# A two-stage convolution with a joint on one Trainium2 core: first samples loaded by phase, warming products split, 414 direct outputs instead of 438, smaller last pieces

## The chip, the cores and the metric

The kernel runs on one core of a Trainium2 chip. The time is the device time of one launch in microseconds (us), the median of three runs. The core's engines are named as in the profile: PE (TensorE; PEld is its weight load), DVE (VectorE), ACT (ScalarE), POOL (GpSimd) and SP (SyncE, which here only issues DMAs). Engines run on their own and wait for each other by semaphores.

## The reference

Two batches of 4000 samples with 512 channels go through two convolutions of 5 taps, each with a GELU and then every second output kept. A joint follows: a product with `w_f`, a sum with a term of `g` for each of 8 labels, tanh, and a product with `w_o`.

```python
B, T, D, K = 2, 4000, 512, 5
U = 8
...
xp = jnp.pad(x, ((0,0),(pad,pad),(0,0)))
for i in range(K):
    h = h + jnp.einsum("btc,cd->btd", xp[:, i:i+T, :], w1[i])
h = _gelu(h)[:, ::2, :]
...
for i in range(K):
    f = f + jnp.einsum("btc,cd->btd", hp[:, i:i+T1, :], w2[i])
f = _gelu(f)[:, ::2, :]
fe = jnp.einsum("btd,de->bte", f, w_f)
ge = jnp.einsum("bud,de->bue", g, w_g)
j = jnp.tanh(fe[:, :, None, :] + ge[:, None, :, :])
return jnp.einsum("btud,dv->btuv", j, w_o)
```

All inputs and the output are bf16. The output has 2 x 1000 x 8 rows of 512.

## The kernel before

**How it is written.** Every operation is recorded in a plan (`Plan`, L69) with what it reads and writes. `edges` finds who must wait for whom. `schedule` (L160) then lays the operations out on the engines by estimated costs, tries up to 300 variations, and `emit` writes each engine's instructions in that order. Operations that carry a "pin" keep their order; for the others PE takes the one recorded first among those that the estimate has ready, and ACT and DVE the one that is due first. All DMAs but two at the end are issued by SP, in the order in which they are recorded. A DMA with an entry in `after` waits until an earlier one has landed, and everything behind it in SP's queue waits with it. An edit of an estimate or of an amount of work thus can move the order of the whole plan.

**First convolution, batch 0.** Its outputs are made in two ways. The first ND = 438 outputs are computed directly: `direct` (L778) multiplies each of the 5 taps, in the order `TAPS` = 0, 4, 2, 1, 3, and accumulates in PSUM banks 0, 2, 4 and 6, one bank for each block of 128 output channels. One call makes 4 x 4 products (4 blocks, 4 parts of the 512 input channels) over `hi - lo` columns. The even taps read the even samples, the odd taps the odd ones. Their input is `eo` (even and odd samples, channels on partitions). It comes from `xr`: two tiles of raw samples, in which each partition holds 4 consecutive samples of 512 channels. `load_xr` (L529) loads tile 0 (128 partitions, 512 KB) and tile 1 (`NR[1]` = 96 partitions, 384 KB). `turn(rt, pp)` (L600) transposes the samples of phase pp (0 even, 1 odd) of tile rt on PE, eight transposes in two groups, and DVE or ACT copies each group from PSUM into `eo`. The first NH = 254 columns need tile 0 alone, so the even taps are split: columns 0 to NH, and NH to ND.

The next outputs of batch 0, and all of batch 1, are made by `Triple` (L661): three outputs together by 9 products instead of 15, from sums and differences of samples and of weights. These sums are made by ACT and DVE (`step` for samples, `w1part` for weights). `Unit` (L711) runs the products of one block of 128 channels of one triple. The first triple covers NF = 186 groups of three outputs, the second NL = 336; ND / 3 + NF + NL is 668 in all. The triples' samples are loaded with a transpose in the DMA, one for each of 6 phases: `xa` for the first (`load_a`, L556, 192 rows in each), `xp` for the others.

**Order of the start.** SP issues `xr` tile 0, `w1` tap 0, `w1` tap 4, then (when tile 0 has landed) `xr` tile 1, then (when tap 0 has landed) `w1` tap 2, `xa` phases 4 and 0, (when tap 4 has landed) `w1` tap 1, `xa` phase 2, (when tile 1 has landed) `w1` tap 3, the other `xa` phases, and then 18 `xp` loads. PE runs NWARM = 7 products over a tile of zeros (`warm_mm`, L591), whose result nobody reads, while the first samples are on their way. Then come the transposes, the direct products, and the units of the triples. `w1part` of DVE begins when taps 0 and 4 are there.

**The end.** The joint's last product is made in blocks of 128 rows. Most blocks go in groups of four by a scheme of seven products (`Seven`, L1086); single blocks left over go by `Plain` (L1063), which multiplies, copies from PSUM (`evict`) and stores. The last lines (L1284 to L1290) run one plain block, the first half (256 columns) of another, the last product `p4` of the last `Seven`, a plain block, and the second half of the other, whose store ACT issues. The program ends when all stores have landed.

Of the kernel before, what the change touches and what calls it, by code (L numbers as in the profile page):

```python
# [12 lines left out]
P = 128  # L13
# [355 lines left out]
def bass_standalone__seq2seq_rnn_t_joint__speech_kernel(  # L369
# [22 lines left out]
    NK = D // P  # L392
    assert (B, T, D, K, U) == (2, 4000, 512, 5, 8)
    T1, T2 = T // 2, T // 4
    NT3 = (T2 + 2) // 3
    ND, NF = 438, 186
    NL = 2 * NT3 - ND // 3 - NF
    assert ND % 6 == 0 and NF % 2 == 0 and NL % 2 == 0
    EW = 16 + 4 * P
# [3 lines left out]
    RING, WIDE, XB = 16, 10, 32  # L403
    BU = B * U
    NT = 512
    NWARM = 7
    TAPS = (0, 4, 2, 1, 3)
    NX = 2

    with ExitStack() as es:  # L410
        cur = [16512]

        def at(name, shape, dtype, offset=None):
            o = cur[0] if offset is None else offset
            b = Buf(nc, name, shape, dtype, o)
            if offset is None:
                cur[0] = (b.end + 31) // 32 * 32
            return b
# [10 lines left out]
        wo_sb = at("wo_sb", [NK, D], BF16)  # L429
        h_off = cur[0]  # L430
        hT = [at(f"hT{b}", [6, NK, HWID], BF16) for b in range(B)]
        xr = [Buf(nc, f"xr{i}", [4, NK, P], BF16, h_off + 16384 + i * 4096) for i in range(NX)]
# [10 lines left out]
        ident = at("ident", [P], BF16)  # L443
# [23 lines left out]
        ost = [at(f"ost{i}", [NT], BF16, h_off + 12288 + i * 1024) for i in range(3)]  # L467
# [13 lines left out]
        ps = Psum(es.enter_context(nc.psum_tensor("acc", [P, 8 * NT], FP32)))  # L481
        block = es.enter_context(nc.Block(no_gpsimd_drain=True))
        pl = Plan(nc)
        sub, add = ALU.subtract, ALU.add

        def vec_cost(o, ins, fast=True):
            bf = fast and all(not v.psum and v.ap.dtype in (BF16, FP16) for v in (o,) + tuple(ins))
            return o.ap.free_size() * (0.52e-3 if bf else 1.04e-3) + 0.065
# [8 lines left out]
        def act(o, i, func, scale=1.0, bias=None):  # L497
            rd = (i,) if bias is None else (i, bias)
            pl.op("act", lambda e: e.activation(o.ap, i.ap, func, scale=scale,  # L499
                                                bias=0.0 if bias is None else bias.ap), rd, (o,),  # L500
                  o.ap.free_size() * 0.833e-3 + (0.05 if i.psum else 0.105 if bias is None else 0.186))

        def mm(o, pairs, start, stop, check=True):

            def fn(e):
                for n, (l, r) in enumerate(pairs):
                    ins = e.matmul(o.ap, lhsT=l.ap, rhs=r.ap, start=start and n == 0,  # L507
                                   stop=stop and n == len(pairs) - 1, skip_group_check=not check)
                return ins
            pl.op("pe", fn, [v for pr in pairs for v in pr], (o,), len(pairs) * max(o.ap.free_size() / 2400 + 0.0028, 0.056))  # L510
# [13 lines left out]
        def load_w(eng, dst, src, slack=0.0):  # L524
            return pl.dma(eng, lambda e: e.dma_start(dst.ap, src), (), (dst,), slack=slack)  # L525

        NR = (P, 16 * -(-(2 * ND + 2 - 4 * P) // 64))

        def load_xr(rt, after=None):  # L529
            n = NR[rt]  # L530
            dst = xr[rt].rows(0, n).map(lambda a: a.rearrange("p r k c -> p (r k c)"))
            src = x[0, 4 * P * rt:4 * (P * rt + n), :].rearrange("(p r) c -> p (r c)", r=4)
            o = pl.dma("sp", lambda e: e.dma_start(dst.ap, src), (), (dst,), nbytes=n * 4096, rate=370e3)  # L533
            if after is not None:
                o.after.append(after.idx)
            return o
# [5 lines left out]
            src = x.rearrange("b t d -> (b t) d")[r0:r0 + 6 * (n - 1) + 1:6, :]  # L542
            return pl.dma("sp", lambda e: e.dma_start_transpose(out=dst.ap, in_=src), (), (dst,), nbytes=n * 2 * D, rate=175e3, slack=slack)

        came = [load_xr(0)]
        act(warm[0:1], warm[1:2], ACT.Gelu_apprx_tanh)

        def load_w1(i, after=None):
            o = load_w("sp", w1_sb[i], w1[i].rearrange("(k c) d -> c k d", c=P))
            if after is not None:  # L550
                o.after.append(after.idx)
            return o
# [3 lines left out]
        def load_a(*phs):  # L556
            for ph in phs:
                load_x6(xa, 0, ph, JA, 0, 16 * -(-(NF + 2) // 16), 0.8)

        came.append(load_w1(TAPS[0]))  # L560
        came.append(load_w1(TAPS[1]))
        came.append(load_xr(1, came[-3]))
        came.append(load_w1(TAPS[2], came[-3]))
        load_a(4, 0)
        came.append(load_w1(TAPS[3], came[-3]))
        load_a(2)
# [24 lines left out]
        def warm_mm(n):  # L591
            z, zz = zero[0:P], zero[:]
            for i in range(n):
                mm(ps.cols(0, NT), [(z, zz)], True, True)
                pl.ops[-1].cost = 0.43

        warm_mm(NWARM)
        psb = ps.h[:, :].bitcast(BF16)

        def turn(rt, pp, cost):  # L600
            n = NR[rt]
            for h in range(2):
                bk = 4 * (rt ^ pp) + 2 * h + 1
                pv = View(psb[:, bk * 1024:bk * 1024 + 4 * n].rearrange("p (r k c) -> p r k c", r=2, k=2), np.array([bk]), True)

                def fn(e, pv=pv, h=h):
                    for k in range(2):
                        for r in range(2):
                            ins = e.transpose(pv.ap[:, r, k, :], xr[rt].h[0:n, 2 * r + pp, 2 * h + k, :], ident.h[0:n, 0:n])  # L609
                    return ins  # L610
                pl.op("pe", fn, (xr[rt][:], ident[:]), (pv,), cost)
                lo = 16 + 2 * P * rt
                o = eo[pp, 2 * h:2 * h + 2, lo:lo + 2 * n].map(lambda a: a.rearrange("p k (c r) -> p k c r", r=2))
                v = pv.map(lambda a: a.rearrange("p r k c -> p k c r"))
                if h or rt:
                    act(o, v, ACT.Copy)
                else:
                    pl.op("dve", lambda e, o=o, v=v: e.tensor_copy(out=o.ap, in_=v.ap), (v,), (o,), vec_cost(o, (v,)))
# [157 lines left out]
        NH = 2 * P - 2  # L776

        def direct(i, lo=0, hi=ND):  # L778
            for m in range(NK):
                mm(ps.cols(2 * m * NT + lo, hi - lo),  # L780
                   [(w1_sb[i, k, m * P:(m + 1) * P], eo[i % 2, k, 15 + i // 2 + lo:15 + i // 2 + hi]) for k in range(NK)],
                   i == TAPS[0] and lo == 0, i == TAPS[-1], False)

        def h_edges(b):
            memset(hT[b][4:6, :, HOFF - 1:HOFF])
            memset(hT[b][:, :, HOFF + NT3:HOFF + NT3 + 2])

        pl.pin = False
        h_edges(0)
        turn(0, 0, 0.43)  # L790
        direct(TAPS[0], 0, NH)
        turn(0, 1, 0.43)
        direct(TAPS[1], 0, NH)
        turn(1, 0, 0.17)
        turn(1, 1, 0.17)
        direct(TAPS[2], 0, NH)
        for i in TAPS[:3]:
            direct(i, NH, ND)
        for i in TAPS[3:]:
            direct(i)  # L800
        for m in range(NK):
            v = ps.cols(2 * m * NT, ND).map(lambda a: a.rearrange("p (q r) -> p r q", r=6))
# [123 lines left out]
        def slot(j):  # L926
            if j < XB:
                return jT, j % RING
            j = (j - XB) % (WIDE + RING)
            return (jX, j) if j < WIDE else (jT, j - WIDE)  # L930
# [8 lines left out]
        def jcols(k, lo, n):  # L939

            buf, j = slot(lo // JB)
            lo = j * JB + lo % JB
            return buf[k, lo:lo + n]
# [82 lines left out]
        H = NT // 2  # L1026

        def take():
            return free.pop(0)

        def evict(eng, o, v):
            if eng is None:
                n = o.ap.free_size()
                pl.flex({"act": (lambda e: e.activation(o.ap, v.ap, ACT.Copy), 0.05 + n * 0.833e-3),  # L1034
                         "dve": (lambda e: e.tensor_copy(out=o.ap, in_=v.ap), 0.065 + n * 1.04e-3)}, (v,), (o,))  # L1035
            elif eng == "act":
                act(o, v, ACT.Copy)
            else:
                pl.op("dve", lambda e: e.tensor_copy(out=o.ap, in_=v.ap), (v,), (o,), vec_cost(o, (v,)))
# [12 lines left out]
        def store(jt, src, key, eng="sp", cl=slice(0, NT)):  # L1052
            lo = c0 = jt * P
            while lo < c0 + P:
                vv = lo // T2
                n = min((vv + 1) * T2, c0 + P) - lo
                b, u, t = vv // U, vv % U, lo % T2
                s = src(lo - c0, lo - c0 + n)
                dst = out[b, t:t + n, u, cl]
                pl.dma(eng, lambda e, s=s, dst=dst: e.dma_start(dst, s.ap), (s,), (), sem_of(key), 2 * n * P * 4)  # L1060
                lo += n

        class Plain:  # L1063
# [8 lines left out]
            def go(self, eng=None):  # L1072
                self.part(slice(0, NT), eng, "sp")

            def half(self, h, eng, queue):
                self.part(slice(h * H, (h + 1) * H), eng, queue)

            def part(self, cl, eng, queue):
                bk = take()
# [170 lines left out]
        plains = [j for j in range(ntile) if not any(q <= j < q + 4 for q in jts)]  # L1250
# [5 lines left out]
        for i, q in enumerate(seven):  # L1256
            p = seven[i - 1] if i else None
            base = min([(p or q).jt] + plains[:1]) * P
            last = i + 1 == len(seven)
            r = []  # L1260
# [23 lines left out]
        assert not conv and not pend and len(plains) == 3, (len(conv), len(pend), plains)  # L1284
        Plain(plains[0]).go()
        end = Plain(plains[2])
        end.half(0, "dve", "sp")
        seven[-1].p4(True)
        Plain(plains[1]).go()
        end.half(1, "act", "act")  # L1290

        pl.emit(block, [(s[0], s[1]) for s in sems.values()])

# [27 lines left out]
```

## Time and profile before

| | us |
|---|---|
| median of 3 runs | 252.72 (252.49 to 252.78) |
| the profiled execution | 252.61 |
| its span, first to last instruction | 250.8 |
| PE busy | 246.1 (98%) |
| ACT busy, DVE busy | 211.1, 209.4 |
| first warming product / first transpose / first direct product | 1.19 / 4.21 / 5.93 |
| first product of the first triple | 22.38 |
| last copy from PSUM starts | 247.61 |
| HBM read and written | 7.73 MB, 16.38 MB |

The span begins with the first instruction and ends with the last; the profiled time holds it and what lies around it. "Busy" of PE says that a product was in the array, not that the array was at its peak: PE's products are pipelined and their ends modelled. What an engine waits for is given by the releaser behind an arrow. A chain of waits, followed back from the last instruction, shows which work ended last at each point; work off that chain costs nothing as long as it stays off it. The weight loads (PEld) have starts that show how fast the products follow each other.

### The profile page before, as it was taken

How to read it: one execution, taken by the hardware profiler on the slowest of the kernel's cores; microseconds unless marked ns; L12 is line 12 of the kernel's file. 1: busy time of each engine (PE TensorE's matmuls, PEld its weight loads, DVE VectorE, ACT ScalarE, POOL GpSimd, SP SyncE). 2: the span in 40 equal slices, each digit the busy share in tenths (PEclk: the TensorE clock that was granted, in tenths of full speed). 3: DMA queues.
4: the chain of work that ended last, by engine and by line, in shares of the span. 5: the costliest groups of instructions: out<-in, count | busy, mean ns of one | idle time of the engine just before them, and what ended most of it. 6: DMA issues, size and time to landing. Idle time of an engine off the chain costs nothing.

```text
span 250.8 us, 5265 instructions
## 1 busy us (share of the span) xinstructions
PE 246.1 (98%) x1947; PEld 183.4 (73%) x1947; DVE 209.4 (84%) x354; ACT 211.1 (84%) x351; POOL 98.8 (39%) x106
## 2 busy tenths in 40 slices
PE   8999999999999999999999999999999999999994
PEld 4887887666666666667556878777788878787882
DVE  2699998966999999398966888777999999987783
ACT  3399998859868867884599999999999999998772
POOL 1000000000000000000006978979799899888840
PEclk9999999999999999999999999999999999999999
DMA  7999999989000043000001043423354554555456
GB/s 241 276 242 195 158 197 179 187 208 293 2 3 0 0 146 109 0 4 0 0 3 42 0 137 111 132 86 104 94 184 142 187 188 158 167 173 185 151 189 210
DMA packets 54455, 31.86 MB, mean 127 GB/s; under 512 B 31390, under 2 KB 54206, under 8 KB 54430
## 3 DMA queue, kind: packets, MB, share of 16 engines
q1 hardware_dynamic: 54142, 31.34, 47.2%
q8 instruction: 15, 0.25, 0.4%
q10 hardware_dynamic: 288, 0.20, 0.3%
q14 instruction: 10, 0.08, 0.1%
HBM read 7.73 MB, written 16.38 MB: 96 GB/s over the span
## 4 chain that ended last, share of the span: by engine, by line
PE 93%; DMA 3%; ACT 2%; DVE 1%; issue 1%; SPq 0%; DVEq 0%
PE acc L507 92%; DMA w_sb<-in_w_dram 3%; ACT row L499 1%; DVE row L494 0%; PE acc L609 0%; DVE acc L621 0%; DVE w_t L494 0%; ACT w_x L499 0%; ACT sd L499 0%; SPq L525 0%; SPq L533 0%; ACT ost L499 0%; DVE sd L494 0%; DVEq L330 0%
## 5 line engine op out<-in xcount | busy, mean ns | idle before, releaser
L494 DVE TENSOR_TENSOR og<-acc,sn 128x512 bf16<-128x512 f32 x84 | 54.9, 682 | 7.9 <-PE acc L507 7.5
L499 ACT ACTIVATE jT<-feT,geT 128x1000 bf16<-128x1000 f32 (+5 forms) x60 | 57.4, 1016 | 0.3 <-DVE feT L494 0.3
L1108 POOL TENSOR_TENSOR ss<-jT 128x512 f16<-128x512 bf16 x33 | 38.4, 1170 | 41.3 <-DVE ss L1108 41.0
L507 PE MATMUL acc<-tw,ss 128*128 128x256 f16 x336 | 46.2, 273 | 0.0
L507 PE MATMUL acc<-row,w_sb 128*128 128x334 bf16 (+2 forms) x224 | 38.9, 296 | 0.2 <-DVE acc L621 0.2
L507 PEld LDWEIGHTS acc<-tw,ss 128*128 128x128 f16 x336 | 32.3, 98 | 7.6 <-ACT sn L1034 0.6
L507 PE MATMUL acc<-wo_sb,jT 128*128 128x256 bf16 (+1 forms) x208 | 33.2, 285 | 0.0
L1034 ACT ACTIVATE sn<-acc 128x512 f32<-128x512 f32 x48 | 29.7, 628 | 3.1 <-PE acc L507 2.3
L1035 DVE COPY sn<-acc 128x512 f32<-128x512 f32 x36 | 24.6, 685 | 7.0 <-PE acc L507 6.6
L507 PEld LDWEIGHTS acc<-row,w_sb 128*128 128x128 bf16 x224 | 21.1, 97 | 9.9 <-DVE acc L621 1.4
L491 POOL MEMSET hT<- 128x8 bf16 (+2 forms) x6 | 0.8, 148 | 63.2 <-ACT hT L499 46.3
L507 PEld LDWEIGHTS acc<-wo_sb,jT 128*128 128x128 bf16 x208 | 20.3, 98 | 5.0
L499 ACT ACTIVATE sd<-acc 128x334 f32<-128x334 f32 (+2 forms) x48 | 20.5, 432 | 2.9 <-PE acc L507 1.7
L499 ACT ACTIVATE hT<-acc 128x334 bf16<-128x334 f32 (+3 forms) x36 | 15.4, 438 | 8.7 <-PE acc L507 8.4
L1108 POOL TENSOR_TENSOR ss<-ss,jT 128x512 f16<-128x512 f16 x19 | 21.9, 1156 | 0.8 <-DVE ss L1108 0.8
L621 DVE SCALAR_TENSOR_TENSOR acc<-acc,sd 128x334 f32<-128x334 f32 (+2 forms) x24 | 11.5, 479 | 9.6 <-PE acc L507 9.5
L494 DVE TENSOR_TENSOR row<-row 128x1336 bf16<-128x1336 bf16 (+2 forms) x24 | 18.8, 792 | 0.0
L499 ACT ACTIVATE jX<-feT,geT 128x1000 bf16<-128x1000 f32 (+3 forms) x20 | 18.4, 968 | 0.0
L507 PE MATMUL acc<-xp,w_t 128*128 128x334 bf16 (+1 forms) x96 | 17.6, 305 | 0.0
L507 PE MATMUL acc<-hT,w_t 128*128 128x334 bf16 x96 | 17.6, 304 | 0.0
L507 PE MATMUL acc<-wo_sb,ss 128*128 128x256 bf16 x112 | 17.3, 273 | 0.0
L507 PE MATMUL acc<-xp,w_x 128*128 128x334 bf16 (+1 forms) x96 | 16.9, 305 | 0.0
(124 smaller groups left out, 494.6 us busy)
## 6 DMA issues: line engine op xcount, KB each, us to landing
out_dram<-og SPq DMA_DIRECT2D x42, 256.0 KB, 2.5
w_sb<-in_w_dram SPq DMA_DIRECT2D x10, 512.0 KB, 5.4
out_dram<-og SPq DMA_DIRECT2D x14, 128.0 KB, 2.1
out_dram<-ost SPq DMA_DIRECT2D x10, 128.0 KB, 1.9
xr<-in_x_dram SPq DMA_DIRECT2D x1, 512.0 KB, 3.4
wf_sb<-in_w_f_dram SPq DMA_DIRECT2D x1, 512.0 KB, 3.8
wg_sb<-in_w_g_dram SPq DMA_DIRECT2D x1, 512.0 KB, 4.8
wo_sb<-in_w_o_dram SPq DMA_DIRECT2D x1, 512.0 KB, 7.2
```

What stands on the lines that cost most here:

```text
L491: pl.op("pool", lambda e: e.memset(v.ap, 0.0), (), (v,))
L494: pl.op(eng, lambda e: e.tensor_tensor(out=o.ap, in0=a.ap, in1=b.ap, op=op), (a, b), (o,), 0.02 + 2.14e-3 * o.ap.free_size() if eng == "po ...
L499: pl.op("act", lambda e: e.activation(o.ap, i.ap, func, scale=scale, bias=0.0 if bias is None else bias.ap), rd, (o,), o.ap.free_size() * ...
L507: ins = e.matmul(o.ap, lhsT=l.ap, rhs=r.ap, start=start and n == 0, stop=stop and n == len(pairs) - 1, skip_group_check=not check)
L621: pl.op(eng, lambda e: e.scalar_tensor_tensor(out=o.ap, in0=a.ap, scalar=f, in1=b.ap, op0=ALU.mult, op1=add), (a, b), (o,), vec_cost(o, (a ...
L1034: pl.flex({"act": (lambda e: e.activation(o.ap, v.ap, ACT.Copy), 0.05 + n * 0.833e-3), "dve": (lambda e: e.tensor_copy(out=o.ap, in_=v.ap) ...
L1035: "dve": (lambda e: e.tensor_copy(out=o.ap, in_=v.ap), 0.065 + n * 1.04e-3)}, (v,), (o,))
L1108: fn = lambda e, o=S[i], x=x, y=y, op=op: e.tensor_tensor(out=o.ap, in0=x.ap, in1=y.ap, op=op)
```

## The change

There are four edits.

- **Amounts.** ND is 414 instead of 438 and NF 194 instead of 186; NL stays 336. From these, `NR[1]` becomes 80 instead of 96, and the `xa` loads have 208 rows instead of 192.
- **Loads by phase.** `load_xr` takes a phase and loads only the two even or the two odd ones of each partition's 4 samples, as rows of 1 KB instead of 4 KB in one run. Even tile 0 goes first. Even tile 1 and tap 2 wait for tap 0. The odd halves of both tiles wait for tap 4; they stand behind tap 2 and ahead of `xa` phase 4 in SP's queue. `turn` now depends on its own phase alone, and DVE makes one copy into `eo` (the first group of the even phase of tile 0) instead of two; ACT makes the other seven.
- **Warming and order on PE.** NWARM is 5, and two more warming products are recorded behind the transposes of the even phase of tile 0. The odd phase of tile 0 is transposed behind tap 2 and the second part of tap 0, instead of ahead of tap 4.
- **The end.** The block that was cut into two halves of 256 columns is cut into 384 and 128 columns. The plain block between is multiplied and copied in two halves of 256 columns, both by DVE, and stored whole.

```diff
-    ND, NF = 438, 186
+    ND, NF = 414, 194
...
-    NWARM = 7
+    NWARM = 5
...
-        def load_xr(rt, after=None):
+        def load_xr(rt, pp, after=None):
             n = NR[rt]
-            dst = xr[rt].rows(0, n).map(lambda a: a.rearrange("p r k c -> p (r k c)"))
-            src = x[0, 4 * P * rt:4 * (P * rt + n), :].rearrange("(p r) c -> p (r c)", r=4)
-            o = pl.dma("sp", lambda e: e.dma_start(dst.ap, src), (), (dst,), nbytes=n * 4096, rate=370e3)
+            dst = xr[rt].rows(0, n, slice(pp, 4, 2)).map(lambda a: a.rearrange("p r k c -> p r (k c)"))
+            src = x[0, 4 * P * rt:4 * (P * rt + n), :].rearrange("(p r) c -> p r c", r=4)[:, pp:4:2, :]
+            o = pl.dma("sp", lambda e: e.dma_start(dst.ap, src), (), (dst,), nbytes=n * 2048, rate=350e3)
...
-        came = [load_xr(0)]
+        came = [load_xr(0, 0)]
...
-        came.append(load_xr(1, came[-3]))
-        came.append(load_w1(TAPS[2], came[-3]))
+        came.append(load_xr(1, 0, came[1]))
+        came.append(load_w1(TAPS[2], came[1]))
+        for rt in range(NX):
+            load_xr(rt, 1, came[2])
         load_a(4, 0)
...
-                pl.op("pe", fn, (xr[rt][:], ident[:]), (pv,), cost)
+                pl.op("pe", fn, (xr[rt][pp:4:2], ident[:]), (pv,), cost)
...
-                if h or rt:
+                if h or rt or pp:
                     act(o, v, ACT.Copy)
...
         turn(0, 0, 0.43)
+        pl.hold = [max(o.idx for o in pl.ops if o.eng == "pe")]
+        warm_mm(2)
+        pl.hold = []
         direct(TAPS[0], 0, NH)
-        turn(0, 1, 0.43)
         direct(TAPS[1], 0, NH)
         turn(1, 0, 0.17)
+        direct(TAPS[2], 0, NH)
+        direct(TAPS[0], NH, ND)
+        turn(0, 1, 0.43)
         turn(1, 1, 0.17)
-        direct(TAPS[2], 0, NH)
-        for i in TAPS[:3]:
+        for i in TAPS[1:3]:
             direct(i, NH, ND)
...
-            def half(self, h, eng, queue):
-                self.part(slice(h * H, (h + 1) * H), eng, queue)
+            def halves(self, eng, queue):
+                for cl in (slice(0, H), slice(H, NT)):
+                    bk = take()
+                    v = ps.cols(bk * NT, H)
+                    mm(v, [(jcols(k, self.jt * P, P), wo_sb[k, cl]) for k in range(NK)], True, True)
+                    evict(eng, ost[self.s][cl], v)
+                    free.append(bk)
+                store(self.jt, lambda a, b: ost[self.s].rows(a, b), ("p", self.s), queue)
...
-        end.half(0, "dve", "sp")
+        end.part(slice(0, 3 * P), "dve", "sp")
         seven[-1].p4(True)
-        Plain(plains[1]).go()
-        end.half(1, "act", "act")
+        Plain(plains[1]).halves("dve", "sp")
+        end.part(slice(3 * P, NT), "act", "act")
```

## The prediction

> **What bounds the kernel now.** I read the page first: how much of the span TensorE (PE) is not busy, and at which clock.
>
> ```profile
> span 250.8 us, 5265 instructions
> PE 246.1 (98%) x1947; PEld 183.4 (73%) x1947; DVE 209.4 (84%) x354; ACT 211.1 (84%) x351; POOL 98.8 (39%) x106
> ```
>
> PE lacks 4.7 us of the span: 1.19 before its first product, about 3.2 behind its last, and so only some 0.3 in between. An edit can gain by less PE work, by PE work of more use in the first 8 us, or behind the last product. Next the chain of waits, in order of time (start, length, what):
>
> ```profile
> 1.65 6.74 DMA w_sb<-in_w_dram
> 8.39 0.05 issue
> 8.43 1.92 PE acc L507 x16
> 10.35 0.68 PE acc L609 x16
> 11.04 13.13 PE acc L507 x116
> ...
> 31.31 216.28 PE acc L507 x1676
> 247.59 0.02 issue
> 247.61 0.38 ACT ost L499
> ```
>
> The start of everything is the landing of tap 4's weights at 8.39. From 8.43 PE is the chain but for 24.17 to 31.31, where ACT and DVE steps of the triples alternate on it. Then the timeline of the first 11 us (start, length, engine, line, work):
>
> ```profile
> 4.18 0.34 SPq L533 DMA_DIRECT2D xr<-in_x_dram  x1
> ...
> 4.21 1.89 PE L609 MATMUL acc<-ident,xr 128*128 128x128 bf16 x16
> 4.85 0.69 DVE L618 COPY eo<-acc 128x512 bf16<-128x512 bf16 x1 [3.72 <-PE acc L609]
> 5.28 0.60 ACT L499 ACTIVATE eo<-acc 128x512 bf16<-128x512 bf16 x1 [3.05 <-PE acc L609]
> 5.66 0.38 SPq L525 DMA_DIRECT2D w_sb<-in_w_dram  x1
> ...
> 5.93 4.42 PE L507 MATMUL acc<-eo,w_sb 128*128 128x254 bf16 x32
> ...
> 8.43 1.64 PEld L507 LDWEIGHTS acc<-eo,w_sb 128*128 128x128 bf16 x16 [0.34 <-DMA w_sb<-in_w_dram]
> ...
> 9.41 0.58 SPq L525 DMA_DIRECT2D w_sb<-in_w_dram  x1
> ```
>
> xr0 lands at 4.18, tap 0's weights at 5.66 (SP waited for them), tap 4's 0.34 after PE wanted them. Weight loads in narrow stretches of the same view give PE's clock in this front:
>
> ```profile
> 6.55 0.36 PEld L507 LDWEIGHTS acc<-eo,w_sb 128*128 128x128 bf16 x2
> 6.76 0.35 PEld L507 LDWEIGHTS acc<-eo,w_sb 128*128 128x128 bf16 x2
> 6.97 0.25 PEld L507 LDWEIGHTS acc<-eo,w_sb 128*128 128x128 bf16 x2
> ```
>
> 254-column products start 0.21 apart until 6.97 and 0.108 apart later: the array runs at half speed until about 7.0, though the page's clock row shows full. So PE time before 7.0 is worth half. Last, stretches of the middle and the end (busy us of PE, PEld, DVE, ACT, POOL; clock, DMA share, GB/s):
>
> ```profile
> 24.40:26.40 2.00, 1.83 (x23) 1.61 (x22) 2.00 (x5) 2.00 (x4) 0.00 (x0) 1.00 1.00 184
> 26.40:28.40 2.00, 2.00 (x27) 2.00 (x26) 2.00 (x6) 2.00 (x4) 0.00 (x0) 1.00 1.15 189
> ...
> 249.00:249.25 0.25, 0.00 (x0) 0.00 (x0) 0.00 (x0) 0.00 (x0) 0.00 (x0) 1.00 1.02 340
> 249.25:249.50 0.25, 0.00 (x0) 0.00 (x0) 0.00 (x0) 0.00 (x0) 0.00 (x0) 1.00 0.97 279
> 249.50:249.75 0.25, 0.00 (x0) 0.00 (x0) 0.00 (x0) 0.00 (x0) 0.00 (x0) 1.00 0.22 58
> ```
>
> DVE has no idle from 8.41 to 38.4 and ACT little: cover for PE is thin there. At the end the DMA engines are full until 249.5.
>
> **Loads by phase.** The engines move about 0.36 MB/us from 2.25 on (slices of 336 to 389 GB/s), and a load counts as landed some 0.7 us after its last byte: 0.52 MB (xr0) are through by 3.5, landed 4.15; 1.05 MB (with w1 tap 0) by 4.9, landed 5.6. The even half of xr0 is 0.26 MB: through by 2.74, landed 3.45. Tap 0's weights: 0.79 MB by 4.2, landed 4.9. Tap 4's: 1.31 MB by 5.7, landed 6.4 to 7.0. Before, they would by the same count (1.57 MB) have landed at 7.1; they came 1.26 later because xr1's 384 KB, issued at 4.18, shared the engines with them. Even xr1 (160 KB) is now issued at 4.9, its bytes flow from about 6, behind tap 4's.
>
> **Warming and tap 0.** Five warming products at 0.427 end at 3.3 (1.19 + 2.13). Eight transposes at 0.107 run 3.47 to 4.33, and two warming products to 5.18. The copies into eo follow the transposes as before, 0.64 (DVE) and 1.07 (ACT) after their start: the ACT one ends at 3.47 + 1.07 + 0.60 = 5.14. Tap 0 starts at 5.19 instead of 5.93; the two warming products lie wholly beside these copies. Until 6.98 it is 1.79 / 0.212 = 8.5 products at half speed, and 7.5 x 0.108 = 0.82 at full speed: end 7.80, and tap 4's weights are there. Tap 4 starts at 7.80 instead of 8.43: **-0.63**. Bounds: if the even half lands no sooner than 4.15, tap 0 starts at 5.93 and ends at 8.09, which still saves the wait: -0.34. If full speed comes after as much product time as now (3.0 warming + 1.05 direct = 4.05), it comes at 6.3, tap 4 starts at 7.46: -0.97. I take the middle, since the trace has full speed at one moment only and shows no cause for another.
>
> [...]
>
> **Work of PE behind that point.** A column costs 0.417 ns (186 columns: 80 ns, four in 0.32; 438 columns: 185 ns, fourteen steps in 2.59). Direct: 5 taps x 16 blocks x 24 columns = 1920 columns, **-0.80**. Triples: 9 x 16 products x 8 columns = 1152, **+0.48**. xr1's 16 transposes have 80 columns instead of 96: 256 columns, **-0.11**. The odd transposes of xr0, 0.86 at half speed ahead of tap 0, now run at full speed behind it: eight of 128 columns; the sixteen of 96 take 0.047 each, so 0.38 to 0.48: **+0.45**. Together +0.02.
>
> **Queue of SP.** SP now waits for tap 4's weights ahead of two odd xr loads, with xa phases 4 and 0, w1 tap 1, xa 2, w1 tap 3, the other xa and all xp loads behind. xa phase 4 goes out at about 7.3 (6.45 + two issues of 0.4) instead of 6.09, w1 tap 1 at 10.2 to 10.8 instead of 9.41, tap 3 near 12.6 instead of 11.30; each xa load has 208 rows instead of 192, 8% of its 1.2 to 1.9. Landing took 4.3 for tap 1 and 5.8 for tap 3: tap 1's weights come at 14.5 to 16.6, tap 3's at 18.4. PE wants them at 7.80 + 1.74 + 0.33 + 1.74 + 1.11 + 0.45 + 0.33 + 2.22 = 15.7, and 2.8 later. Odd xr0 (landed about 9.7) is wanted at 12.7, even xr1 (7.1) at 9.5. So it fits with 0 to 1.2 to spare; cost 0, bounds 0 and 0.9. xp loads are 1.6 later; xp phase 2 now lands at 25 and ACT first takes it at 27.78.
>
> **DVE and ACT.** DVE begins its weight sums when tap 4's weights land, 1.4 to 2.0 earlier; its triples are 4% wider, under 0.4. ACT takes both copies of the odd xr0 phase (2 x 0.60, inside its full stretch now) and saves 4 x 0.07 on xr1. Its head start, since it follows DVE's sums, is about 1.6, its addition about 1.0. The two waits of PE there (0.17 and 0.28) may vanish or double; I take them unchanged: 0, bounds -0.45 and +0.5.
>
> **The end.** The same columns of PE; 128 instead of 256 columns in the last ACT copy, 0.38 - 0.11 = 0.27. But from 246.8 to 249.55 the engines drain 0.92 MB without a gap, and the bytes are the same: 0, bounds -0.15 and +0.1. [...]
>
> **Sum.** -0.63 + 0.02 = -0.61. The profiled execution took 252.61 (span 250.8 and 1.8 around it), 0.11 under the median 252.72. 252.72 - 0.61 = **252.1**.
>
> **The rivals.** *DVE and ACT keep the end of the first triples* (same). For: DVE full to 38.4, later xa and xp loads. Against: their own earlier start. If the wait at 31.31 ends when it does now, nothing of the front survives: 252.4 to 252.9.
>
> *SP's new wait makes tap 1's weights late* (slower). If tap 4's weights still land near 8.4, tap 4 starts as now, SP issues odd xr at 8.45 and w1 tap 1 at 12.6 (8.45 + 0.8 + 3.3), landing at 16.9 to 18.4, wanted at 16.4: a wait of 0.5 to 2.0 on PE, 253.2 to 254.7. It decides from a landing of tap 4's weights later than about 7.8. For: they came 1.26 later than bytes alone say. Against: what shared the engines then is issued later and is 160 KB.
>
> [...]
>
> *More gain*: full speed at 6.3 and no waits at 26 and 31: -0.34 - 0.45, 251.4 to 251.8. *The change does not do what it says* (half rows of 1 KB land no earlier): -0.34 + 0.02, 252.4.
>
> **How the numbers follow.** Forecast 0.39, more gain 0.09, DVE and ACT 0.31, no earlier landing 0.02, late tap 1 0.13, late clock 0.06. Faster by over 0.2% (under 252.2; about what this measurement can tell from no change) 0.39 + 0.09 = 0.48; within 0.31 + 0.02 = 0.33; slower 0.13 + 0.06 = 0.19. The range reaches from 251.4 (more gain) into the late tap 1, 253.2; outside are the late clock and most of that case, under 0.2. The forecast's own range is 251.7 to 252.2.
>
> **What would show it.** Right: transposes at 3.5 and tap 0 at 5.2 in the timeline, no wait of PEld before tap 4, tap 4 at 7.8, loads half as dense until 7.0, the first xa product near 21.4 (22.38 now), its last products 0.6 earlier than now. Wrong: PEld waiting for w_sb at taps 1 or 3; DVE as releaser of PE for over 0.5 between 24 and 33; products 0.21 apart beyond 7.

## The result, and the profile after

The changed kernel takes 254.41 us (median of 7 runs, 253.73 to 256.32); the kernel before, on the same chip in turn with it, 253.14 (252.49 to 253.46). The ratio is 1.0076, with a 95% interval from 1.0054 to 1.0097: slower by 0.8%, where 0.24% faster was forecast. The profiled execution took 254.35 us, 1.74 more than the profiled one of before.

The first lines of the page after, span and busy times:

```profile
span 252.6 us, 5280 instructions
PE 244.9 (97%) x1951; PEld 182.8 (72%) x1951; DVE 209.8 (83%) x354; ACT 211.0 (84%) x352; POOL 98.9 (39%) x106
```

PE is busy 1.2 us less than before, and the span is 1.8 longer: PE now lacks 7.7 us of it instead of 4.7. So time without a product was added. (Of the 1.2, the columns are 0.43 by the prediction's count. The rest is mostly work of the front that ran at half speed before: tap 0's products were 0.21 apart until 6.97 and are 0.11 apart now, and the odd transposes of tile 0 run at full speed too: the sixteen of both tiles take 0.90, where the sixteen of tile 0 took 1.89.) The chain of waits says who stands in for PE; first its shares of the span by engine, then two landings early on it, from the same chain in order of time (start, length, what):

```profile
PE 71%; DVE 16%; DMA 5%; SPq 3%; issue 3%; ACT 1%; ACTq 0%; DVEq 0%
```

```profile
2.11 5.80 DMA w_sb<-in_w_dram
...
13.92 6.07 DMA w_sb<-in_w_dram
```

Before, one landing (tap 4's) stood ahead of PE on the chain. Now it is followed by SP's queue from 7.93 on and by a second landing, that of w1 tap 3, at 19.99. From there the chain runs through DVE's steps to 28.41, where PE waits for DVE. SP's timeline in the first 15 us (start, length, engine, line, work) has the reason:

```profile
0.73 0.70 SPq L533 DMA_DIRECT2D xr<-in_x_dram  x1
...
6.58 0.66 SPq L533 DMA_DIRECT2D xr<-in_x_dram  x1
7.29 0.59 SPq L525 DMA_DIRECT2D w_sb<-in_w_dram  x1
...
12.02 0.58 SPq L525 DMA_DIRECT2D w_sb<-in_w_dram  x1
...
13.92 0.58 SPq L525 DMA_DIRECT2D w_sb<-in_w_dram  x1
```

The half of xr0 takes 0.70 to issue (the whole one took 0.39). SP waits for the landing of tap 0's weights, and only then does it go on: even xr1 at 6.58, tap 2 at 7.29, w1 tap 1 at 12.02 (9.41 before), tap 3 at 13.92 (11.30). Tap 2 stood behind this wait before too, but xr1 went out ahead of the wait, at 4.18, and the wait ended at 5.66. Now even xr1 stands behind the wait as well, and the wait ends 0.9 later. The same in PE's weight loads (idle before them, and its releaser, in brackets):

```profile
4.02 0.77 PEld L611 LDWEIGHTS acc<-ident,xr 128*128 128x128 bf16 x8 [1.42 <-DMA xr<-in_x_dram]
...
6.78 3.41 PEld L507 LDWEIGHTS acc<-eo,w_sb 128*128 128x128 bf16 x32 [1.80 <-issue]
...
11.43 2.83 PEld L507 LDWEIGHTS acc<-eo,w_sb 128*128 128x128 bf16 x32 [0.81 <-DMA w_sb<-in_w_dram]
14.23 0.83 PEld L611 LDWEIGHTS acc<-ident,xr 128*128 128x128 bf16 x16
...
28.41 0.28 PEld L507 LDWEIGHTS acc<-row,w_sb 128*128 128x128 bf16 x4 [0.77 <-DVE acc L623]
```

Even xr0 lands at 4.02, 0.16 sooner than the whole tile did, not 0.73 sooner as forecast (3.45). Tap 0 starts at 6.78, later than before (5.93). Taps 0 and 4 then run in one stretch at full speed (32 products in 3.41), so tap 4 starts near 8.5. Tap 2 waits 0.81 for its weights, until 11.43 (10.83 before, with no wait), and the odd transposes of both tiles follow at 14.23 with nothing beside them to hide them.

The reason behind the late weights shows in stretches of half a microsecond (busy us and instructions of PE, PEld, DVE, ACT, POOL; granted clock, DMA share, GB/s). The kernel before:

```profile
2.00:2.50 0.50, 0.50 (x3) 0.21 (x2) 0.00 (x0) 0.22 (x2) 0.00 (x0) 1.00 0.69 238
...
3.00:3.50 0.50, 0.50 (x3) 0.17 (x2) 0.00 (x0) 0.00 (x0) 0.00 (x0) 1.00 0.90 344
...
7.00:7.50 0.50, 0.50 (x6) 0.45 (x5) 0.00 (x0) 0.00 (x0) 0.00 (x0) 1.00 1.05 205
```

and the kernel after:

```profile
2.00:2.50 0.50, 0.50 (x3) 0.21 (x2) 0.00 (x0) 0.22 (x2) 0.00 (x0) 1.00 0.40 72
...
3.00:3.50 0.50, 0.50 (x2) 0.00 (x0) 0.00 (x0) 0.00 (x0) 0.00 (x0) 1.00 0.79 193
3.50:4.00 0.50, 0.00 (x1) 0.00 (x0) 0.00 (x0) 0.00 (x0) 0.00 (x0) 1.00 0.36 102
...
7.00:7.50 0.50, 0.50 (x7) 0.44 (x6) 0.00 (x0) 0.00 (x0) 0.00 (x0) 1.00 0.08 27
7.50:8.00 0.50, 0.50 (x7) 0.45 (x5) 0.06 (x1) 0.00 (x0) 0.00 (x0) 1.00 0.00 0
```

The first bytes flow later than before (72 GB/s against 238 at 2.0 to 2.5), and then the rate falls twice. By the sums of the stretches the half tile (0.26 MB) is through near 3.3; the weights of tap 0, issued from 1.49 on, stand behind it, and the rate is 102 GB/s at 3.5 to 4.0. By 7.0 the engines have moved 1.30 of the 1.31 MB that were issued in the first 2.7 us; SP has been waiting for the landing of tap 0, and of what it issues at 6.58 and 7.29 nothing flows before 8.0 (0 GB/s at 7.5 to 8.0). Summed over the twelve stretches from 2.0 to 8.0, the engines moved 1.94 MB before and 1.31 MB after.

Behind the front, PE's waits from 8 to 40 us by group in the kernel after (total us, times, longest us), its two largest; before they were 0.7 for DVE and 0.3 for a landing:

```profile
PEld acc L507 <- DVE acc L623: 1.0, 2, 0.8
PEld acc L507 <- DMA w_sb<-in_w_dram: 1.0, 2, 0.8
```

The time in one account, after against before: tap 4 starts 0.09 later. From there to the first xa product it takes 14.36 instead of 13.95: 0.81 for tap 2's weights, less 0.46 for columns and transposes (-0.80 - 0.11 + 0.45, the prediction's terms), and 0.06 not accounted for. The first xa product thus starts at 22.88 (22.38), 0.50 later. The last xp product starts at 100.83 (99.36), 1.46 later. Of the 0.96 added on the way, 0.48 are the triples' columns, and 0.48 are left for waits; on the weight loads the waits are 0.18, 0.77 and 0.25 up to 30 us, against 0.39 and 0.28 up to 32 us before. Behind that, PE waits 0.49 for ACT at 105.25, in the second convolution, where before it has no such wait; this adds 0.32. The first product of the joint starts 1.8 later (134.4), and the span ends 1.8 later. In the tail nothing changed: ACT's last copy starts at 249.44 and the last bytes leave about 1.9 later, as before (247.61, 249.55).

### The profile page after: what moved, and what is told of

It is laid out like the page before. It is cut to its first block, busy times and chain, and to the rows that moved or that the text cites. A ratio compares the mean times of both kernels' runs of the same rounds, so it can differ in the third digit from the quotient of the medians.

```text
span 252.6 us, 5280 instructions
## 1 busy us (share of the span) xinstructions
PE 244.9 (97%) x1951; PEld 182.8 (72%) x1951; DVE 209.8 (83%) x354; ACT 211.0 (84%) x352; POOL 98.9 (39%) x106
## 4 chain that ended last, share of the span: by engine, by line
PE 71%; DVE 16%; DMA 5%; SPq 3%; issue 3%; ACT 1%; ACTq 0%; DVEq 0%
PE acc L507 71%; DMA w_sb<-in_w_dram 5%; DVE row L494 3%; DVE ws L623 2%; DVE ssum L494 2%; SPq L543 2%; DVE hT L494 2%; DVE acc L623 1%; DVE xp L494 1%; DVE sd L494 1%; DVE w_t L494 1%; DVE xa L494 1%; ACT row L499 1%; DVE w_sb L494 1%; SPq L533 1%
```

## The experiments

Two theories stood against each other. First: the *loads by phase* cost the time, since they leave the engines empty (27 and 0 GB/s at 7.0 to 8.0) and hold up SP's queue. Second: the *order on PE* costs it, since the odd transposes were moved from a place where PE waited for weights anyway (0.34 for tap 4's) to one where it has none to wait for, and since five warming products leave PE idle ahead of the first samples (0.52 in the profile after). Third in line stood the amounts, the end, and the order of steps, which a search with random moves (L209) plans for all engines anew whenever anything in the kernel changes. A change of 0.2% is near what these comparisons can tell.

**The changed kernel with whole loads (e1).** The loads of xr and what they wait for are those of before; amounts, order on PE and end are those of after.

```diff
...
-        came = [load_xr(0, 0)]
+        came = [load_xr(0)]
...
-        came.append(load_xr(1, 0, came[1]))
-        came.append(load_w1(TAPS[2], came[1]))
-        for rt in range(NX):
-            load_xr(rt, 1, came[2])
+        came.append(load_xr(1, came[-3]))
+        came.append(load_w1(TAPS[2], came[-3]))
```

> The changed kernel, but with both xr tiles loaded whole and waited for as before; amounts, warming, order on PE and end as changed. Theory L (the loads by phase cost the time: tap 0's weights came at 6.55 instead of 5.62, and the DMA engines stood idle from 7.0 to 8.1): the first xa product comes near 22.2, and the time falls from the changed kernel's 254.4 to within 0.5 us of before (253.1). Theory A (the amounts 414 and 194 cost it: wider triples where DVE is full): most of the loss stays, over 254.0. Theory E (the end): as A.

Measured: 1.0067 [1.0047, 1.0087], 254.07 against 252.45. Nearly the whole loss stays without the loads by phase, so the first theory alone does not hold. In its profile PE waited for tap 4's weights until 8.88, the first xa product came at 22.6 (22.2 was expected), and ACT held PE up by 1.0 in the triples.

**The changed kernel with its waits one step earlier (e2).** Even xr1 and tap 2 wait for even xr0 instead of tap 0, the odd halves for tap 0 instead of tap 4.

```diff
-        came.append(load_xr(1, 0, came[1]))
-        came.append(load_w1(TAPS[2], came[1]))
+        came.append(load_xr(1, 0, came[0]))
+        came.append(load_w1(TAPS[2], came[0]))
         for rt in range(NX):
-            load_xr(rt, 1, came[2])
+            load_xr(rt, 1, came[1])
```

> The changed kernel with other waits alone: even xr tile 1 and tap 2 wait for even tile 0 (landed 4.02) instead of tap 0 (6.55), the odd halves for tap 0 instead of tap 4. Theory L in the form 'the wait for tap 0 empties the DMA engines': no empty stretch at 7 to 8, tap 2 lands at about 9 to 10 instead of 11.43, so PE's wait of 0.8 before tap 2 goes and the later loads come 1.5 to 2.5 us sooner; the time falls by 1 us or more, to about 253.3; tap 0's weights may come some tenths later. In the form 'more, shorter rows make every issue and landing slow': tap 0 still at 6.5, and under 0.5 us gained. Theory A: no change beyond 0.3.

Measured: 1.0052 [1.0032, 1.0072], 253.67 against 252.45. One of its stretches (columns as above):

```profile
7.00:7.50 0.50, 0.50 (x5) 0.32 (x3) 0.00 (x0) 0.00 (x0) 0.00 (x0) 1.00 1.13 244
```

The second empty stretch is gone (244 GB/s for 27), so SP's wait for tap 0 made it; tap 2 started at 10.90 without a wait, and the first xa product at 22.4. By the ratios about a third of the loss went, though the intervals overlap, and the steps of ACT and DVE stand in another order here too, which alone can move the changed kernel by 0.2% (e7, below). So the gain of a third isn't shown. 0.32 to 0.72% stay, so a large part of the loss lies elsewhere.

**Amounts alone, end alone, both (e3, e4, e6).** The kernel before with ND = 414 and NF = 194; with the new end; with both.

```diff
-    ND, NF = 438, 186
+    ND, NF = 414, 194
```

> The kernel before with 414 direct outputs and 194 triples alone. By PE's columns 0.43 less work (-0.80 + 0.48 - 0.11): theory L expects 0 to -0.5 against before (253.1). Theory A expects +0.7 or more, with longer waits of PE for DVE between 24 and 34 us.

```diff
...
-        end.half(0, "dve", "sp")
+        end.part(slice(0, 3 * P), "dve", "sp")
         seven[-1].p4(True)
-        Plain(plains[1]).go()
-        end.half(1, "act", "act")
+        Plain(plains[1]).halves("dve", "sp")
+        end.part(slice(3 * P, NT), "act", "act")
```

> The kernel before with the new last pieces alone. Theories L and A expect within 0.2 us of before, since the DMA engines drain the same bytes to the end. Theory E (the 256-byte rows and the four more products cost): +0.5 or more, with a longer stretch from PE's last product (247.6) to the last instruction.

> The kernel before with the amounts and the end of the changed kernel together; loads, warming and order on PE as before. Theory O: within 0.4 of before, so that the whole loss of the kernel with whole loads (+0.67%) is the order's. Rival (amounts and end cost together): +0.8 or more.

Measured: amounts 0.9994 [0.9979, 1.0009], end 1.0009 [0.9994, 1.0024], both 0.9990 [0.9973, 1.0007]. None of them can be told from no change, and none explains a loss of 0.8%. A gain of the amounts, 0.43 us or 0.17% by the columns counted in the prediction, fits the intervals but isn't shown.

**The order alone (e5).** The kernel before with the changed order on PE, five warming products ahead and two behind, and ACT making seven of the eight copies into eo.

```diff
-    NWARM = 7
+    NWARM = 5
...
-                if h or rt:
+                if h or rt or pp:
...
         turn(0, 0, 0.43)
+        pl.hold = [max(o.idx for o in pl.ops if o.eng == "pe")]
+        warm_mm(2)
+        pl.hold = []
         direct(TAPS[0], 0, NH)
-        turn(0, 1, 0.43)
         direct(TAPS[1], 0, NH)
         turn(1, 0, 0.17)
-        turn(1, 1, 0.17)
         direct(TAPS[2], 0, NH)
-        for i in TAPS[:3]:
+        direct(TAPS[0], NH, ND)
+        turn(0, 1, 0.43)
+        turn(1, 1, 0.17)
+        for i in TAPS[1:3]:
```

> The kernel before with the order on PE alone: 5 warming products and 2 behind the even transposes, the odd transposes of tile 0 behind tap 2 and the second part of tap 0, and all but one copy into eo by ACT. Loads, amounts and end as before. Theory O (the order costs: two copies of 0.60 now lie in ACT's full stretch and 0.45 of transposes behind tap 4, with no earlier landing to pay for them): +1 us or more against before, with PE waiting longer for ACT or DVE between 22 and 40 us. Theory L (loads): within 0.3 of before. If the parts only cost together: +0.3 to +0.8.

Measured: 1.0056 [1.0035, 1.0076], 253.89 against 252.68. So the order makes a loss on its own, with the loads, amounts and end of before. PE's weight loads of its profiled execution (253.07, its fastest):

```profile
8.11 1.64 PEld L507 LDWEIGHTS acc<-eo,w_sb 128*128 128x128 bf16 x16 [0.26 <-DMA w_sb<-in_w_dram]
...
10.94 2.97 PEld L507 LDWEIGHTS acc<-eo,w_sb 128*128 128x128 bf16 x32 [0.37 <-DMA w_sb<-in_w_dram]
13.89 0.51 PEld L609 LDWEIGHTS acc<-ident,xr 128*128 128x128 bf16 x8
```

PE is 0.3 earlier at tap 4 than before, and then waits for tap 2's weights: the lead is lost to the next landing. The odd transposes at 13.89 to 14.36 are the bill: from the start of tap 2 to the first xa product it takes 11.78 (10.94 to 22.72) instead of 11.36 (10.83 to 22.19, by weight loads). This part repeats: it is 11.78 in all three profiles with the new order and the amounts and loads of before (e5, e9, e13), and 11.33 to 11.36 in the five with the old order (before, e4, e8, e10, e14). Nor does tap 2 start sooner for it, at 10.68 to 11.63 against 10.39 to 11.88. The longer waits for ACT or DVE that theory O expected between 22 and 40 us are not there (0.20 and 0.23 on the weight loads, against 0.39 and 0.28 before).

**Another plan (e7, e8).** The search of both kernels with other random numbers.

```diff
-            rng = np.random.default_rng(tried)
+            rng = np.random.default_rng(tried + 1000)
```

> The changed kernel with other random numbers in the planner's search and nothing else: another order on DVE and ACT. Theory P (the loss is the luck of the plan found): it moves by 0.8 us or more from the changed kernel's ratio of 1.0076, either way. Theories O and L: the ratio stays within 0.0025 of 1.0076.

> The kernel before with other random numbers in the planner's search and nothing else. Theory P: +0.8 us or more against before, as the plan of before would then be a lucky one. Theories O and L: within 0.4.

Measured: the changed kernel 1.0095 [1.0064, 1.0127], the kernel before 1.0006 [0.9989, 1.0023]. The changed kernel loses with both plans and the kernel before with neither, so the loss is not the bad luck of one plan. Two plans of each say little on how far a plan can move the time.

**The order with seven warming products (e9).** As the order alone, but with seven products ahead of the first samples and two behind.

```diff
-    NWARM = 5
+    NWARM = 7
```

> The order of e5 with 7 warming products ahead of the transposes instead of 5 (and 2 behind them). The order alone cost 1.0056, 1.4 us, of which 0.45 are the odd transposes at full speed behind tap 4. Theory G (the clock: PE idles from 3.3 to 4.0 with 5 products, and full speed then comes late in some executions): falls to +0.3 to +0.7 us against before. Theory O (moved transposes and copies alone): stays at +1.0 to +1.8.

Measured: 1.0030 [1.0013, 1.0047], 253.55 against 252.67. In its profile the weights came late (tap 4 waited until 9.00, tap 2 until 11.63), and the odd transposes stood at 14.58 for 0.51. So 0.3% remain with the order when PE is warmed as before. That is 0.8 to 0.9 us, between the ranges that the two theories gave.

**Five warming products alone (e10).** The kernel before with NWARM = 5 and nothing else.

> The kernel before with 5 warming products instead of 7 and nothing else. PE then idles from 3.3 until the samples land at 4.2. Theory G: +0.5 to +1.2 us, with the 254-column products of tap 0 still 0.21 apart in the profile, or even later ones. Theory O: within 0.3, since nothing waits for a warming product.

Measured: 1.0017 [1.0001, 1.0033], 253.06 against 252.67. Weight loads of its profile, in narrow stretches, by which the clock was read in the prediction:

```profile
8.70 0.36 PEld L507 LDWEIGHTS acc<-eo,w_sb 128*128 128x128 bf16 x2
8.91 0.29 PEld L507 LDWEIGHTS acc<-eo,w_sb 128*128 128x128 bf16 x2
```

Products stay 0.21 apart until 8.91, where they did until 6.97 before: tap 0 and tap 4 took 4.87 for their 32 products, and tap 2 started at 11.60 instead of 10.83. PE is idle for 0.74 ahead of the first transpose at 4.25, and in this execution full speed came 1.9 later. The cost is small in the mean, some 0.4 us, again between the two forecasts; the interval barely leaves 1.

**The changed kernel with seven and four (e11).** NWARM = 7 and four warming products behind the transposes.

```diff
-    NWARM = 5
+    NWARM = 7
...
-        warm_mm(2)
+        warm_mm(4)
```

> The changed kernel with 7 warming products ahead of and 4 behind the even transposes, so that PE has no idle stretch before tap 0. Theory G: falls from 1.0076 to about 1.004 and the executions spread less (253.7 to 256.3 before). Theories L and O: stays within 0.002 of 1.0076.

Measured: 1.0112 [1.0090, 1.0134], 255.51 against 252.67, the slowest of all. Its front was the faster one (tap 0 at 6.03, tap 4 without a wait, the first xa product at 22.5 instead of 22.88), but ACT held PE up for 1.5 before 60 us and 1.5 after, and DVE for 0.8 and 0.7. Neither forecast held. The plan of ACT's and DVE's steps is another one than in the changed kernel, so this run can't separate the warming from the plan and says nothing on the warming.

**Second parts ahead of tap 2 (e12).** The kernel before, but xr1 waits for tap 0 instead of xr0, so that it goes out at 5.61 instead of 4.18, and the second parts of taps 0 and 4 run ahead of a whole tap 2.

```diff
-        came.append(load_xr(1, came[-3]))
+        came.append(load_xr(1, came[1]))
...
-        direct(TAPS[2], 0, NH)
-        for i in TAPS[:3]:
+        for i in TAPS[:2]:
             direct(i, NH, ND)
+        direct(TAPS[2])
```

> The kernel before with two edits: xr tile 1 waits for tap 0 instead of tile 0, so that its 384 KB no longer share the engines with tap 4's weights, and the second parts of taps 0 and 4 come ahead of tap 2, which then runs whole. If the landing of tap 4's weights (8.4 to 9.4 in the profiles so far, with 0.3 to 1.8 us of wait on PE) is what sets the front: tap 4 starts near 8.0 without a wait, and the time falls by 0.5 to 0.9 us. If the sum of bytes up to tap 2 sets it: within 0.3 of before.

Measured: 1.0018 [0.9998, 1.0038], 253.09 against 252.67. PE's weight loads:

```profile
7.70 1.64 PEld L507 LDWEIGHTS acc<-eo,w_sb 128*128 128x128 bf16 x16 [0.23 <-DMA w_sb<-in_w_dram]
...
11.03 0.72 PEld L609 LDWEIGHTS acc<-ident,xr 96*128 96x128 bf16 x16 [1.68 <-DVE wu L621]
```

Tap 4 starts at 7.70, 0.73 sooner, which is what the forecast wanted of its front. (The edit need not be why: with the loads of before, tap 4's weights landed anywhere between 7.4 (e4) and 9.4 (e8).) Nothing comes of it: xr1, issued later, lands only near 11.0, and PE stands idle for 1.68 (the wait is put down to a DVE step here; PE's own line in the same trace has the landing of xr). What one load gained here (0.73), the next paid (1.68). At 0.4 us over before the run is near the "within 0.3" of a front bound by the sum of its bytes and far from the forecast gain, but it does not show that the bytes alone bind.

**The order with DVE's copy, and the copy alone (e13, e14).** The order with seven products, DVE making the copy of the odd phase as before; and the kernel before with that copy given to ACT. The lines are those of the first; the second has them the other way round.

```diff
-                if h or rt or pp:
+                if h or rt:
```

> The kernel of e9 (order on PE as changed, 7 and 2 warming products), but with DVE making the first copy of the odd phase as before, so ACT has one copy of 0.60 less in its full stretch. Theory C (the added copies on ACT make up what the moved transposes do not): from 1.003 to about 1.001. Theory T (the moved transposes alone, 0.47 of PE time behind tap 4): unchanged at 1.002 to 1.003.

> The kernel before with the second DVE copy into eo given to ACT, order and all else as before: the copy lies near 6 us, where ACT is idle. Theories C and T: within 0.3 us of before.

Measured: 1.0040 [1.0026, 1.0054] and 1.0000 [0.9984, 1.0017]. No cost of the copy can be told from these, and giving it back saves nothing. In the weight loads of the first of the two, tap 2 at 10.68 is 0.15 ahead of before, the first xa product at 22.46 is 0.27 behind: 11.78 between them again, 0.42 more than before.

**The loads by phase on that order (e15).** The order with seven and two warming products, and the loads by phase with their waits; amounts and end as before.

> The kernel of e9 (order as changed, 7 and 2 warming products, amounts and end as before) with the loads by phase and their waits added. Theory L (the loads cost by themselves: 1.4 us with empty engines at 7 to 8, tap 2 late by 0.8): 1.003 rises to 1.005 or more. Theory N (the loads neither win nor lose, since tap 2's weights come at 10.7 to 11.6 either way): 1.002 to 1.004. The forecast (the loads win 0.6): 1.001 or less.

Measured: 1.0087 [1.0062, 1.0111], 254.68 against 252.51. Against the same order with whole loads (1.0030 and 1.0040) the loads by phase cost about half a per cent, as theory L said, and the intervals do not overlap. From PE's weight loads:

```profile
11.08 2.97 PEld L507 LDWEIGHTS acc<-eo,w_sb 128*128 128x128 bf16 x32 [1.00 <-DMA w_sb<-in_w_dram]
```

The signs are those of the changed kernel: the engines moved 8 GB/s at 7.0 to 7.5, tap 2 waits 1.00 for its weights, SP issues w1 tap 1 at 11.43 and tap 3 at 13.32, some 2 later than before, and DVE, which follows the late weights and samples, holds PE up by 1.20 at 29.43, in the triples. The wait for tap 2 repeats: it is 0.81 to 2.12 in all four profiles with loads by phase in which even xr1 and tap 2 wait for tap 0 (after, e7, e11, e15), and nothing shows in e2, which has the same loads without that wait. With whole loads it is 0.37 at most.

No version tried here is faster than the kernel before by more than the comparison can tell; amounts and end together come nearest (0.9990).

## Why the prediction was wrong

**The step that failed is the first term, -0.63: "tap 4 starts at 7.80 instead of 8.43".** It counted the bytes ahead of a load, divided by 0.36 MB/us (the stretches of before from 2.5 to 7.0 have 315 to 399 GB/s), and added 0.7 for the landing, as if the rate held. In the kernel before it held where the first load (0.52 MB) gave way to the weights behind it (344 GB/s at 3.0 to 3.5, 358 at 3.5 to 4.0). The half began to flow later and was through near 3.3, and then the rate fell (193 GB/s, then 102), though the next load had been issued from 1.49 on. Even xr0 landed at 4.02 (forecast 3.45), tap 0's weights just before 6.58 (4.9), tap 4's at 7.91 (6.4 to 7.0), and tap 4 started near 8.5, so the term was +0.09 on its own place. The 0.7 for a landing did not hold either: by the stretches, 0.79 MB (the half tile and tap 0) were through by about 5.4, 1.2 ahead of tap 0's landing. That would fit if the two weight loads shared the engines, which no row here separates. The bound that was set for "lands no sooner" (-0.34) was no bound, since it let only the samples be late and not the weights behind them. Nor is it shown that xr1's bytes made tap 4's weights late before: in the kernels with the loads of before they landed at 7.4 to 9.4, and the xa transposes, issued from 6.09 on, may have held them up as well (the rate of before is 205 and 197 GB/s from 7.0 to 8.0).

**The wait went to the next load.** The prediction had tap 2's weights in time without a row for it, and looked for a late load at taps 1 and 3. Tap 2 waited 0.81, and 0.81 to 2.12 in all four profiles with the same loads and waits. The second parts run ahead of tap 2 (e12) are alike at another place: there a lead of 0.73 at one tap was lost to the next landing.

**"+0.45" for the odd transposes was right in size and had no payer.** They took 0.47 behind tap 2 in the order alone, and 11.78 instead of 11.36 lies between tap 2 and the first xa product. The place they left held no time on the path to gain: PE had to wait for weights there in any case (for tap 4's, 0.23 to 1.81 in nine of the twelve profiles with whole loads). With the gain of 0.63 gone, this term is what the order costs with seven warming products: 1.0030 and 1.0040, or 0.8 to 1.0 us, of which the 0.42 is the part that the profiles show.

**Warming.** "Seven as five and two" was taken as free. Five alone cost 0.17% [0.01, 0.33], and the order with five 1.0056 against 1.0030 with seven, with intervals that overlap. The prediction gave a late clock a chance of 0.06; no run shows what a late clock costs by itself, and five products alone cost some 0.4 us in the mean. Its sign, products 0.21 apart beyond 7, is in the profile of five products alone (until 8.91), and e2's came late too (near 7.7, an estimate from 32 weight loads in 3.88 where 3.41 is full speed); in the profile of the changed kernel it is not there (full speed from 6.78 on), nor in those of e1, e5 and e7. Nor does any run show that full speed comes after a set amount of product time, as the bound of -0.97 supposed: with the same seven products ahead it came anywhere from 4.3 to 6.97.

**SP's queue, "cost 0, bounds 0 and 0.9".** w1 tap 1 was issued at 12.02 (forecast 10.2 to 10.8) and tap 3 at 13.92 (12.6). The rival "SP's new wait makes tap 1's weights late" had the right condition, a landing of tap 4's weights later than 7.8, and the right time (253.2 to 254.7), but the wrong place, so its time fits partly by chance: tap 1 came in time and PE waited 0.20 for tap 3. Two other things hurt. The wait for tap 0, which now holds even xr1 as well as tap 2 and ends 0.9 later, made tap 2 wait 0.81; that went when SP's waits stood one step earlier (e2). And tap 3's weights, held up in SP's queue from tap 4's landing on, reached DVE late: the chain runs from 7.93 over their landing at 19.99 to PE's wait of 0.77 at 28.41.

**DVE and ACT, "0, bounds -0.45 and +0.5".** Between the first xa and the last xp product 0.48 was added beyond the columns, at the upper bound: the head start that was to pay did not come, since it hung on the same early landing. The wait for ACT at 105.25, 0.32 more, lies behind these products, where the prediction had no term.

**What was right.** PE's columns, as far as the profile tells: the terms -0.80, -0.11, +0.45 and +0.48 leave 0.06 open in the account above. And the end: the tail of the stores set it, and smaller pieces with rows of 256 B moved the time by no more than these runs can tell (1.0009 [0.9994, 1.0024]); no run shows the +0.1 that the prediction set as its bound there, and this interval ends at 0.6 us.

In sum: the forecast was -0.61, the profiled execution gave +1.74. Of the difference of 2.35, tap 4's start is 0.72 (8.52 against 7.80), tap 2's weights 0.81, the waits in the triples 0.48, the wait for ACT at 105.25 0.32; 0.02 is left. This is the account of two single executions.

**What stays open.** The parts do not add up: the order with five (0.56%), the loads by phase on top of it with seven (0.5%), and 0.76% for all. On the changed kernel the loads by phase cost only 0.1% (1.0076 against 1.0067, overlapping), on the order with seven products 0.5%. Late data and a late clock may hide each other: with five products alone, at half speed until 8.91, PE did not wait for tap 4's weights, which DVE took at 8.22, and before it waited 0.34. But that split is argued, as only profiled executions show it, and the others show nothing but their time. The profiles do show where the parts meet. From the first xa product to the end of the execution it takes 229.7 to 230.4 in the nine with the amounts of before and whole loads, three of them with the new order; 231.0 with the loads by phase on that order (e15). With the new amounts, which add 0.48 of columns there, it is 230.2 and 230.8 in the old order (e3, e6), 231.5 in the changed kernel and 231.7 in it with whole loads (e1). So in these executions the new order alone lost its time in the front, and behind the front time was lost with the loads by phase, or with order and amounts together. Why the latter lose it with whole loads (ACT held PE up by 1.0 in e1) stays open.

## What to carry to other kernels

Splitting a first load so that its first half lands sooner did not work here, as the half landed 0.16 sooner and the rate behind it fell to 102 GB/s: count what is issued and not yet through at each moment, not only the bytes ahead. Work that lies where an engine waits for data anyway (0.34 for tap 4's weights here) can be free there, and moving it can cost its full price, as the odd transposes did here (0.42 from tap 2 to the first xa product); ask of every gain in a front which landing comes next. A wait put on an issuing queue is paid by what stands behind it in that queue: here SP's wait for tap 0 ended 0.9 later, and w1 tap 1, with two more loads ahead of it, went out at 12.02 instead of 9.41.

## What the runs showed of the hardware

- A load of 512 KB as 128 rows of 4 KB took 0.39 to issue; 256 KB as 256 rows of 1 KB took 0.70, and landed 0.16 sooner. Over all profiles the first weight load on these samples started at 3.95 to 4.13 with the half and at 4.00 to 4.24 with the whole, so half of the bytes gained about 0.1 in the mean.
- The moment of full speed differs from one profiled execution to the next: the first sixteen transposes took 1.07 with the amounts alone, 1.29 with the end alone and 1.89 before. Full speed came near 4.3 and 4.8 in the first two (estimates from these lengths, at 0.107 for a transpose at half speed and half of that at full) and at 6.97 before: 2.7 apart, with the same seven warming products ahead. With five it came at 8.91. The granted clock read 1.00 in the rows of before from the start, and 0.998 to 1.0 as the mean of each of these executions.
- Tap 4's weights landed between 7.3 and 9.4 and tap 2's between 10.3 and 12.6 over the profiles of these kernels, so one profile of a front bound by landings says little about the next execution.
